# Attention and gated convolution on one core: the order of ReLU and PSUM copies in a step, and the step in which v is loaded

## The chip, the core and the metric

The kernel runs on one core of a Trainium2 chip. The metric is the device time of one execution in microseconds, as the median of several executions. The engines are TensorE (PE; its weight loads are shown as PEld), VectorE (DVE), ScalarE (ACT), GpSimd (POOL) and SyncE (SP), which issues nearly all DMAs. Each engine works through its own queue in order, and a DMA that waits in SP's queue holds up those behind it.

## What is computed

The inputs are q, k and v of shape (4, 8, 576, 64), that is 4 batches of 8 heads, and the weights of a two-layer block. In float32:

```python
q_rot, k_rot = (rotate(q), rotate(k))
scores = scale * np.matmul(q_rot, k_rot.transpose(0, 1, 3, 2))
attn = softmax(scores)                     # over the 576 keys
x = np.matmul(attn, v)                     # heads side by side: (4, 576, 512)
h = np.maximum(x @ w_in, 0.0)              # (4, 576, 1024)
conv_out = sum(conv_w[k] * hp[:, k:k + 576, :] for k in range(3))
out = (h * (1 / (1 + np.exp(-conv_out)))) @ w_out
```

`rotate` is the rotary position turn of the two halves of a head, and `hp` is `h` with a row of zeros on either side.

## The kernel before

The work goes by pairs of heads. There are 16 pairs, and a pair p has five steps, n = 5p to 5p + 4, one for each block of 128 queries (the fifth has 64 queries of both heads). A step multiplies q and k of its block (`emit_S`, L260), reduces the negated maximum on DVE (L268), takes the exponential on ACT (L272), and in the following step PE turns the result `st` round (`emit_T`, L320) into the two tiles `tp`, from which ACT makes two big copies into `pt` (L339, recorded at the helper's line L198, 128x512). Of 576 keys 512 are treated so; the remaining 64 of each head are turned by `emit_Trem` (L357), one block in each of the four steps after the first of a pair. It writes columns 320 to 383 of both PSUM tiles `pm` of the step (`m_pair`), and from there two small copies of 128x64 go into row block 8 of `pt`. They are DVE's, recorded at L200. Five steps after its first, a pair is multiplied with v (`emit_E`, L388): two halves, each into columns 0 to 289 of one `pm` tile, evacuated by ACT (L398).

Up to step 25 PE does attention only, and the weights are converted beside it. From step 26 (`WIDE`) on, the two-layer block is mixed in. Two PSUM tiles `pm` belong to a step, and they are taken anew in the next, so whatever writes them first in a step waits for the last reader of the step before. `UNITS` gives steps with units of the first layer (`emit_M1`, L421): one unit in steps 26 to 34, two in 36, 38, 41, 43, 46, 48 and so on. A unit ends with ReLU on ACT (L429), then convolution on DVE (L433, L435), tanh on ACT (L441), the gate on DVE (L444), and a split into two parts on ACT and POOL (L452, L453). `HALVES` gives the 18 steps with half a second matmul (`m2_half`, L523), whose sum is put together from both tiles by ACT (L537) and DVE (L538). After step 80 comes a tail with the rest of the two layers (L421 and L503 on the tiles `mt`).

What sets the order is a table written by hand: `at(n, rank, fn)` puts a function into step n, and within a step the functions run by rank, equal ranks in the order in which they were entered. Each function issues its instructions to the engines' queues as it runs. `onpe` lists the ranks after which deferred work (`defer`, `tick`) gets its turn. The ranks that matter here, from step 26 on:

- 0: `emit_S`; 0.2: the maximum; 0.3: the convolution of the unit entered last in the step before; 0.45: the transposes of q and k on DVE (L233, L236, L242); 1: `emit_T`; 1.1: `emit_Trem`; 1.5: the exponentials
- 1.6: the two big copies of `tp`; 1.7 and 2.7: the normalisation (L402) and, deferred, its split (L406, L407)
- 2: the units of the first layer; 2.5: the convolution of a first unit of two; 2 and 3: the halves of the second matmul
- 5: the small copies of `pm`; 10: `emit_E`; 18: the rotation of q and k on POOL (L189, L192); 19: loads of q, k (L148 to L150) and v (L160, L161)

Loads of q and k for pair p stand in step n - 10 from step 25 on, and each has one buffer, so it waits until DVE has transposed the pair before. The load of v stands in step n + 3, for use in step n + 5.

Of the kernel before, what the change touches and what calls it, by code (L numbers as in the profile page):

```python
# [20 lines left out]
def attention_moe_kernel(ctx, tc, q, k, v, w_in, conv_w, w_out, tab, tabx, out):  # L21
# [52 lines left out]
    late = {"tail": False, "u": 0}  # L74
# [13 lines left out]
    def t_tile():  # L88
        return psum["t"].tile([128, 512], F32, tag="t", name="tp")

    def after(fn):
        if "m" in psum or late["n"] + 1 == WIDE:
            fn()
        else:
            at(late["n"] + 1, 0.35, fn)

    def spare(n):
        a = free["at"]
        if "m" in psum or late["n"] + 1 == WIDE:
            return t_tile()[:, 0:n]  # L100
        assert a + n <= 960
        free["at"] = a + n
        return free["ps"][:, a:a + n]
# [3 lines left out]
    def m_pair():  # L107
        if pair["n"] != late["n"]:
            pair.update(n=late["n"], ps=[psum["m"].tile([128, 512], F32, tag="m", name="pm") for _ in range(2)], k=0)
        return pair["ps"]  # L110
# [30 lines left out]
    def load(p, part):  # L141
        b, hp = divmod(p, NPB)
        x = raw[p, part] = p1.tile([128, S // 32, 2, 32], F32, tag="r" + part, name="r" + part)
        for h in range(2):
            y = (q if part == "q" else k)[b, 2 * hp + h].rearrange("(c i) d -> i c d", i=32)
            r0 = slice(64 * h, 64 * h + 32)
            r1 = slice(64 * h + 32, 64 * h + 64)
            nc.sync.dma_start(out=x[r0].rearrange("i c e d -> i c (e d)"), in_=y)  # L148
            nc.sync.dma_start(out=x[r1, :, 0, :], in_=y[:, :, 32:64])
            nc.sync.dma_start(out=x[r1, :, 1, :], in_=y[:, :, 0:32])  # L150
# [3 lines left out]
    def load_v(p):  # L154
        if p == 0:
            nc.vector.memset(vrem, 0.0)
        b, hp = divmod(p, NPB)
        t = vmain[p] = p1.tile([128, 2, 4, D], F32, tag="vm", name="vm")
        for h in range(2):
            nc.sync.dma_start(out=t[:, h], in_=v[b, 2 * hp + h, 0:512, :].rearrange("(t p) d -> p t d", p=128))  # L160
            nc.sync.dma_start(out=vrem[64 * h:64 * h + 64, h, :], in_=v[b, 2 * hp + h, 512:S, :])  # L161
# [34 lines left out]
    def evac(eng, out, in_, sc=None):  # L196
        if eng == "A" or "m" not in psum:
            nc.scalar.activation(out=out, in_=in_, func=AF.Copy, scale=1.0 if sc is None else sc)  # L198
        elif sc is None:
            nc.vector.tensor_copy(out, in_)  # L200
        else:
            nc.vector.tensor_scalar(out=out, in0=in_, scalar1=sc, scalar2=None, op0=ALU.mult)
# [110 lines left out]
    def emit_T(p, s, h=None):  # L313
        if not h:
            tps[p] = [t_tile() for _ in range(2)]
        ps = tps[p]

        def turn(k, x, r):
            i = slice(64 * r, 64 * r + 64)
            nc.tensor.transpose(ps[r][:, 64 * k:64 * k + 64], x[i], idf[i, i])  # L320

        if s == 4:
            st = strem[p % 2]
            for t in range(4):
                for r in range(2):
                    turn(t, st[:, 128 * t:128 * t + 128], r)
            for r in range(2):
                turn(4, st[:, 512 - 64 * r:640 - 64 * r], r)
            evac("A", pt[:, 0:9:2, 512:S], ps[0][:, 0:320].rearrange("p (k c) -> p k c", k=5))
            evac("A", pt[:, 1:8:2, 512:S], ps[1][:, 0:256].rearrange("p (k c) -> p k c", k=4))  # L330
            evac("A", pt[64:128, 8, 512:S], ps[1][64:128, 256:320])
        else:
            for t in range(4):
                for r in range(2):
                    turn(2 * t + h, ST[p, s][:, h, 64 * h + 128 * t:64 * h + 128 * t + 128], r)
            def out():
                for r in range(2):
                    c = 128 * s + 64 * r
                    evac("A", pt[:, 0:8, c:c + 64], ps[r].rearrange("p (k c) -> p k c", k=8))  # L339

            if h and "m" in psum:
                at(late["n"], 1.6, out)
            elif h:
                out()

    def emit_Trem(p, s):
        x = ST[p, s].rearrange("p h k -> p (h k)")[:, 512:640]
        dst = pt[:, 8, 128 * s:128 * s + 128]
        if "m" not in psum:
            ps = spare(128)  # L350
            nc.tensor.transpose(ps, x, idf)
            after(lambda: evac("V", dst, ps))
            return
        for r in range(2):
            i = slice(64 * r, 64 * r + 64)
            ps = m_pair()[r][:, 320:384]
            nc.tensor.transpose(ps, x[i], idf[i, i])  # L357
            at(late["n"], 5, lambda dst=dst[:, i], ps=ps: evac("V", dst, ps))

    rb = {}  # L360

# [284 lines left out]
    WIDE = 26  # L646
    UNITS = {n: 1 for n in (26, 27, 28, 29, 31, 32, 33, 34)}
    UNITS.update({n: 2 for n in (36, 38, 41, 43, 46, 48, 51, 53, 56, 58, 61, 63, 66, 69, 71, 74, 77, 79)})
    HALVES = [37, 39, 42, 44, 47, 49, 52, 54, 57, 59, 62, 64, 67, 68, 72, 73, 76, 78]
    plan = {}  # L650
    onpe = (0, 0.2, 0.5, 1, 2, 3, 4, 10)
    engines = {nc.tensor.engine, nc.vector.engine, nc.scalar.engine, nc.gpsimd.engine, nc.sync.engine}

    def at(n, rank, fn):
        plan.setdefault(n, []).append((rank, len(plan.get(n, [])), fn))

    def emit():
        with tc.manual_schedule(engines=engines):
# [17 lines left out]
            for p in range(1, NP):  # L676
                n = STEPS * p
                for i, part in enumerate("qk"):
                    if p > 1:
                        at(n - 10 if n - 10 >= WIDE - 1 else n - 9 + 2 * i, 19, lambda p=p, part=part: load(p, part))  # L680
                    early = n - 10 >= WIDE - 1
                    at(n - 8 + i if early else max(n - 6 + i, 0) if p > 1 else 0, 18, lambda p=p, part=part: rope(p, part))
                    at(n - 5 if early else max(n - 4 + 2 * i, 2), 0.45, lambda p=p, part=part: emit_TQ(p, part))
                at(n + 3, 19, lambda p=p: load_v(p))
            for p in range(NP):
                n = STEPS * p
                for s in range(STEPS):
# [30 lines left out]
            for n, k in UNITS.items():  # L718
                for i in range(k):
                    blk, f = divmod(late["u"], NF)  # L720
                    late["u"] += 1
                    at(n, 2, lambda blk=blk, f=f, last=i == k - 1: emit_M1(blk, f, last))
            for i, n in enumerate(HALVES):
                for k, u in enumerate(m2_half(i // 2, i % 2)):
                    at(n, 2 + k, u)
            n = -1
# [30 lines left out]
            last = LASTB - 1  # L757
# [7 lines left out]
            for u in seq + second + m2_units(t, B * S // 128):  # L765
                u()
                tick()

    emit()


# [48 lines left out]
```

## Time and profile before

| what | us |
|---|---|
| median of 3 runs | 515.12 |
| the three runs | 515.41, 511.5, 515.12 |
| the profiled execution | 510.98 |
| its span, first to last instruction | 509.1 |
| PE busy in the span | 463.4 (91%) |
| DVE busy | 368.3 (72%) |
| ACT busy | 316.4 (62%) |
| POOL busy | 301.6 (59%) |

Times in the profile count from the start of the span. A row of the timeline reads: start, duration, engine, line and operation, output<-inputs by the program's names, shapes, how many instructions are merged, and in brackets the idle time of that engine before it and what ended it. A matmul on PE overlaps its neighbours, so PE can be busy all the time. Steps can be found by their score matmuls: step 26 begins near 127.8 us, step 36 near 179.9, step 47 near 242.3, step 48 near 246.8 and step 49 near 252.0; from 212.6 us on the steps of one pair of heads take 26.65 us.

### The profile page before, as it was taken

To read this page: it belongs to the slowest core of one execution; us is meant where nothing else is said; L and a number is where in the kernel's file an instruction comes from. 1 tells how busy PE (TensorE), PEld (TensorE's weight loads), DVE (VectorE), ACT (ScalarE), POOL (GpSimd) and SP (SyncE) were. 2 spreads that over 40 slices of the span, in tenths; PEclk is the share of its full clock that TensorE was granted. 3 is DMA by queue.
4 is the path that set the end of the run, shared out by engine and by line. 5 is a ranking of instruction groups with operands and counts; after the bars stand their busy time and mean duration, and the time that the engine had idled before them with its cause. 6 is when DMAs were issued, how large, how long until landed. Compare 5 with 4: busy or idle time off the path is not lost.

```text
span 509.1 us, 12329 instructions
## 1 busy us (share of the span) xinstructions
PE 463.4 (91%) x4572; PEld 365.8 (72%) x4572; DVE 368.3 (72%) x731; ACT 316.4 (62%) x839; POOL 301.6 (59%) x479
## 2 busy tenths in 40 slices
PE   1879779796879979999999999999999999999997
PEld 1346446454657758787878796979787878899986
DVE  5699888997496958686877777786776475567931
ACT  2588768786485837676768586767677664234510
POOL 3699978999936667566584838392922122223520
PEclk9979897998999999999999999999999999999999
DMA  8976955843331517160807080716101110100011
GB/s 219 184 142 144 203 135 146 205 114 72 72 71 42 100 32 121 48 116 13 152 14 149 13 147 18 137 26 121 42 25 46 35 36 25 41 23 22 0 48 56
DMA packets 140559, 42.71 MB, mean 84 GB/s; under 512 B 132156, under 2 KB 135252, under 8 KB 140500
## 3 DMA queue, kind: packets, MB, share of 16 engines
q1 hardware_dynamic: 139156, 41.54, 38.8%
q8 instruction: 36, 0.59, 0.5%
q10 hardware_dynamic: 1344, 0.39, 0.3%
q14 instruction: 23, 0.19, 0.1%
HBM read 37.12 MB, written 4.79 MB: 82 GB/s over the span
## 4 chain that ended last, share of the span: by engine, by line
PE 46%; DVE 21%; ACT 16%; POOL 8%; DMA 5%; issue 3%; SPq 2%; DVEq 0%; ACTq 0%; POOLq 0%
PE mt L503 10%; PE pm L388 9%; ACT st L272 8%; PE pm L523 7%; PE sp L260 6%; PE mt L421 6%; DVE negm L268 6%; ACT pt L198 5%; DVE c L435 4%; PE pm L421 3%; POOL rk L189 2%; DMA rq<-q 2%; PE tp L320 2%; POOL rq L189 2%; DVE c L433 2%
## 5 line engine op out<-in xcount | busy, mean ns | idle before, releaser
L268 DVE TENSOR_REDUCE negm<-sp 128x1 f32<-128x576 f32 x144 | 102.1, 745 | 29.3 <-PE sp L260 22.0
L272 ACT ACTIVATE st<-sp,negm 128x576 f32<-128x576 f32 x128 | 93.8, 739 | 38.5 <-DVE negm L268 38.0
L453 POOL TENSOR_TENSOR g<-c,g 128x288 fp32r<-128x288 f32 (+4 forms) x88 | 54.3, 639 | 90.7 <-ACT g L452 90.4
L260 PE MATMUL sp<-kT,qT 64*128 64x288 f32 (+4 forms) x556 | 103.1, 472 | 4.8 <-DVE kT L236 2.8
L198 ACT ACTIVATE pt<-tp 128x512 f32<-128x512 f32 (+3 forms) x176 | 84.1, 530 | 7.4 <-PE tp L320 6.9
L435 DVE SCALAR_TENSOR_TENSOR c<-rr,cw,c 128x288 f32<-128x288 f32 x128 | 78.6, 614 | 4.5
L421 PE MATMUL pm<-xT,winh 128*128 128x290 f32 x352 | 74.5, 305 | 0.0
L260 PEld LDWEIGHTS sp<-kT,qT 64*128 64x128 f32 (+1 forms) x556 | 49.2, 179 | 24.4 <-issue 13.2
L407 POOL TENSOR_TENSOR xT<-xn,xT 128x290 fp32r<-128x290 f32 x32 | 27.9, 879 | 65.5 <-ACT xT L406 65.5
L189 POOL TENSOR_TENSOR rq<-rq,tabt 128x192 f32<-128x192 f32 x90 | 57.6, 675 | 13.7 <-DMA rq<-q 13.7
L189 POOL TENSOR_TENSOR rk<-rk,tabt 128x192 f32<-128x192 f32 x90 | 58.7, 685 | 7.8 <-DMA rk<-k 7.8
L320 PEld LDWEIGHTS tp<-idf,st 64*128 64x128 f32 x1024 | 43.3, 140 | 24.8 <-ACT st L272 13.9
L320 PE MATMUL tp<-idf,st 64*128 64x64 f32 x1024 | 49.1, 228 | 9.9 <-ACT st L272 9.6
L421 PEld LDWEIGHTS pm<-xT,winh 128*128 128x128 f32 x352 | 56.2, 189 | 1.8
L523 PE MATMUL pm<-wouth,g 64*128 64x256 f32 x576 | 56.5, 281 | 0.0
L388 PE MATMUL pm<-pt,vm 128*64 128x290 f32 x368 | 51.3, 411 | 3.5 <-DVE pt L200 1.7
L433 DVE TENSOR_SCALAR c<-rr,cw 128x288 f32<-128x288 f32 x64 | 29.4, 460 | 34.1 <-ACT rr L429 34.1
L523 PEld LDWEIGHTS pm<-wouth,g 64*128 64x128 f32 x576 | 52.6, 186 | 0.0
L421 PE MATMUL pm<-xT,winl 128*128 128x290 f32 x176 | 52.0, 296 | 0.0
L523 PE MATMUL pm<-woutl,g 64*128 64x256 f32 x288 | 49.5, 276 | 0.0
L444 DVE SCALAR_TENSOR_TENSOR c<-c,rr 128x288 f32<-128x288 f32 x64 | 38.0, 615 | 9.4 <-ACT c L441 9.4
L441 ACT ACTIVATE c<-c 128x288 f32<-128x288 f32 x64 | 28.3, 442 | 24.7 <-DVE c L435 24.5
(108 smaller groups left out, 888.5 us busy)
## 6 DMA issues: line engine op xcount, KB each, us to landing
rq<-q SPq DMA_DIRECT2D x30, 144.0 KB
rq<-q SPq DMA_DIRECT2D x60, 72.0 KB
rk<-k SPq DMA_DIRECT2D x30, 144.0 KB
rk<-k SPq DMA_DIRECT2D x60, 72.0 KB
w<-moe_w_in SPq DMA_DIRECT2D x8, 512.0 KB
vm<-v SPq DMA_DIRECT2D x32, 128.0 KB
w<-moe_w_out SPq DMA_DIRECT2D x8, 512.0 KB
rb<-rd SPq DMA_DIRECT2D x16, 144.0 KB
```

The costliest lines, as they stand in the source:

```text
L189: nc.gpsimd.tensor_tensor(out=y, in0=y, in1=tabt[:, a:a + 3], op=ALU.mult)
L198: nc.scalar.activation(out=out, in_=in_, func=AF.Copy, scale=1.0 if sc is None else sc)
L260: nc.tensor.matmul(out=out, lhsT=qt[64 * h:64 * h + 64, c], rhs=kt[64 * h:64 * h + 64, a:a + n], start=True, stop=True)
L268: reds.setdefault((p, s), []).append(lambda: nc.vector.tensor_reduce(out=nm, in_=sc, axis=AX.XY if len(sc.shape) == 3 else AX.X, op=ALU.ma ...
L272: lambda: nc.scalar.activation(out=dst, in_=sc, func=AF.Exp, bias=nm, scale=1.0, accum_out=sm)
L320: nc.tensor.transpose(ps[r][:, 64 * k:64 * k + 64], x[i], idf[i, i])
L388: nc.tensor.matmul(out=xp[64 * h:64 * h + 64, :], lhsT=vmain[p][:, h, i, :] if i < 4 else vrem[:, h, :], rhs=pt[:, 2 * i + h if i < 4 else ...
L421: nc.tensor.matmul(out=ps[:, 0:XW], lhsT=w[:, kk, fs], rhs=xT[:, xs, e, :], start=(i == 0), stop=(i == n - 1))
L435: nc.vector.scalar_tensor_tensor(out=c, in0=r[:, j + e:j + e + HS], scalar=cw[:, 8 * e + f:8 * e + f + 1], in1=c, op0=ALU.mult, op1=ALU.add,)
L453: nc.gpsimd.tensor_tensor(out=lo, in0=c[:, o:o + n], in1=hi.bitcast(F32), op=ALU.subtract)
L503: nc.tensor.matmul(out=ops[tt][:, 0:width], lhsT=g_tile(tt, f, e), rhs=w[:, f, cols], start=(f == 0 and i == 0), stop=(f == NF - 1 and i = ...
L523: nc.tensor.matmul(out=ps[r][:, 0:256], lhsT=g_tile(tt, f, e)[rows], rhs=w[rows, f, cols], start=(f == 0 and i == 0), stop=(f == NF - 1 an ...
```

## The change

The first-layer units of a step with two get ranks 2 and 2.4 in place of 2 and 2, and the big copies of such a step move from 1.6 to 2.2, between the two units. The small copies go from DVE to ACT, at the same rank 5, except in step 26, where they get rank 11, behind `emit_E`. The load of v moves from step n + 3 to n + 2 for the pairs from the sixth on. `onpe` gets the new rank 2.4. In `evac`, "A" is ACT and "V" is DVE.

```diff
@@ -339,7 +339,7 @@
                     evac("A", pt[:, 0:8, c:c + 64], ps[r].rearrange("p (k c) -> p k c", k=8))
 
             if h and "m" in psum:
-                at(late["n"], 1.6, out)
+                at(late["n"], 2.2 if UNITS.get(late["n"]) == 2 else 1.6, out)
             elif h:
                 out()
 
@@ -355,7 +355,7 @@
             i = slice(64 * r, 64 * r + 64)
             ps = m_pair()[r][:, 320:384]
             nc.tensor.transpose(ps, x[i], idf[i, i])
-            at(late["n"], 5, lambda dst=dst[:, i], ps=ps: evac("V", dst, ps))
+            at(late["n"], 5 if late["n"] > WIDE else 11, lambda dst=dst[:, i], ps=ps: evac("A", dst, ps))
 
     rb = {}
 
@@ -648,7 +648,7 @@
     UNITS.update({n: 2 for n in (36, 38, 41, 43, 46, 48, 51, 53, 56, 58, 61, 63, 66, 69, 71, 74, 77, 79)})
     HALVES = [37, 39, 42, 44, 47, 49, 52, 54, 57, 59, 62, 64, 67, 68, 72, 73, 76, 78]
     plan = {}
-    onpe = (0, 0.2, 0.5, 1, 2, 3, 4, 10)
+    onpe = (0, 0.2, 0.5, 1, 2, 2.4, 3, 4, 10)
     engines = {nc.tensor.engine, nc.vector.engine, nc.scalar.engine, nc.gpsimd.engine, nc.sync.engine}
 
     def at(n, rank, fn):
@@ -681,7 +681,7 @@
                     early = n - 10 >= WIDE - 1
                     at(n - 8 + i if early else max(n - 6 + i, 0) if p > 1 else 0, 18, lambda p=p, part=part: rope(p, part))
                     at(n - 5 if early else max(n - 4 + 2 * i, 2), 0.45, lambda p=p, part=part: emit_TQ(p, part))
-                at(n + 3, 19, lambda p=p: load_v(p))
+                at(n + (2 if n >= WIDE - 1 else 3), 19, lambda p=p: load_v(p))
             for p in range(NP):
                 n = STEPS * p
                 for s in range(STEPS):
@@ -719,7 +719,7 @@
                 for i in range(k):
                     blk, f = divmod(late["u"], NF)
                     late["u"] += 1
-                    at(n, 2, lambda blk=blk, f=f, last=i == k - 1: emit_M1(blk, f, last))
+                    at(n, 2 + 0.4 * i, lambda blk=blk, f=f, last=i == k - 1: emit_M1(blk, f, last))
             for i, n in enumerate(HALVES):
                 for k, u in enumerate(m2_half(i // 2, i % 2)):
                     at(n, 2 + k, u)
```

What this does to the queues is shown at three places. A name like `rr_1718` is the result of one ReLU, `tp` the tile of the big copies, `pm` that of units, halves and small copies.

The first is ACT in the steps with half a second matmul and two units that follow each other (47 and 48), before:

```order
L272 ACTIVATE st,sums<-sp,negm 128x576 x2
L198 ACTIVATE pt<-tp 128x8x64 x2
L537 ACTIVATE oh<-pm 128x256
L406 ACTIVATE xT<-xn 128x290
L441 ACTIVATE c<-c 128x288
L406 ACTIVATE xT<-xn 128x290
L272 ACTIVATE st,sums<-sp,negm 128x576 x2
L198 ACTIVATE pt<-tp 128x8x64 x2
L429 ACTIVATE rr_1718<-pm 128x289
L429 ACTIVATE rr_1719<-pm 128x289
L452 ACTIVATE g<-c 128x288 x2
```

and with the change:

```order
L198 ACTIVATE pt<-tp 128x8x64 x2
L537 ACTIVATE oh<-pm 128x256
L406 ACTIVATE xT<-xn 128x290
L198 ACTIVATE pt<-pm 128x64 x2
L441 ACTIVATE c<-c 128x288
L406 ACTIVATE xT<-xn 128x290
L272 ACTIVATE st,sums<-sp,negm 128x576 x2
L429 ACTIVATE rr_1718<-pm 128x289
L198 ACTIVATE pt<-tp 128x8x64 x2
L429 ACTIVATE rr_1719<-pm 128x289
L198 ACTIVATE pt<-pm 128x64 x2
L452 ACTIVATE g<-c 128x288 x2
```

The first ReLU went ahead of the big copies, and two small copies from `pm` came in behind the second ReLU, and in the step before behind the first split L406. On DVE the small copies stood between the convolution and the maximum of the same two-unit step:

```order
L433 TENSOR_SCALAR c<-rr_1718,cw 128x288
L435 SCALAR_TENSOR_TENSOR c<-rr_1718,cw,c 128x288 x2
L200 COPY pt<-pm 128x64 x2
L268 TENSOR_REDUCE negm<-sp 128x1
L433 TENSOR_SCALAR c<-rr_1719,cw 128x288
```

With the change the row of L200 is gone there and everywhere, and the others keep their order.

The second place is ACT in step 26 and the beginning of step 27, before:

```order
L429 ACTIVATE rr_1716<-pm 128x289
L398 ACTIVATE xn<-pm 128x290
L272 ACTIVATE st,sums<-sp,negm 128x576 x2
L198 ACTIVATE pt<-tp 128x8x64 x2
L429 ACTIVATE rr_1717<-pm 128x289
L441 ACTIVATE c<-c 128x288
```

and with the change:

```order
L429 ACTIVATE rr_1716<-pm 128x289
L398 ACTIVATE xn<-pm 128x290
L198 ACTIVATE pt<-pm 128x64 x2
L272 ACTIVATE st,sums<-sp,negm 128x576 x2
L198 ACTIVATE pt<-tp 128x8x64 x2
L429 ACTIVATE rr_1717<-pm 128x289
```

The small copies of step 26 stand behind the evacuation of the product with v (L398).

The third place is SP's queue from the loads of step 25 to the loads of v for step 30. These rows are the same before and with the change:

```order
L148 DMA rk<-k 32x18x64
L149 DMA rk<-k 32x18x32
L150 DMA rk<-k 32x18x32
L148 DMA rk<-k 32x18x64
L149 DMA rk<-k 32x18x32
L150 DMA rk<-k 32x18x32
L160 DMA vm<-v 128x4x64
L161 DMA vr<-v 64x64
L160 DMA vm<-v 128x4x64
L161 DMA vr<-v 64x64
L370 DMA rd<-rt 9x32 x4
```

No other DMA stands between steps 27 and 28, so the load of v keeps its place in the queue, and so it does for the pairs after it; only for the last three pairs does a load of v now stand ahead of one output DMA (L539) that it followed before, since there a step with an output lies between.

## Rows read from the trace of the kernel before

**Rows 1.** The head of the page.

```profile
span 509.1 us, 12329 instructions
```

**Rows 2.** Windows: stretch, length, busy PE, PEld, DVE, ACT, POOL; clock, DMA share, GB/s.

```profile
212.60:345.80 133.20, 130.24 (x1531) 109.81 (x1530) 101.72 (x215) 92.64 (x243) 83.49 (x129) 1.00 0.42 78
```

**Rows 3.** Waits, whole span: engine, line waited for: us in total, times, longest.

```profile
PE pm L357 <- DVE pt L200: 7.6, 10, 1.8
...
PE pm L388 <- DVE pt L200: 1.7, 1, 1.7
...
PE pm L388 <- DMA vm<-v: 1.4, 1, 1.4
```

**Rows 4.** Timeline of PE, rows with idle time before them.

```profile
133.12 2.17 PE L388 MATMUL pm<-pt,vm 128*64 128x290 f32 x16 [1.74 <-DVE pt L200]
...
146.14 0.40 PE L357 MATMUL pm<-idf,st 64*128 64x64 f32 x2 [1.09 <-DVE pt L200]
...
151.24 2.73 PE L388 MATMUL pm<-pt,vm 128*64 128x290 f32 x15 [1.42 <-DMA vm<-v]
...
186.40 1.71 PE L260 MATMUL sp<-kT,qT 64*128 64x288 f32 x7 [1.28 <-ACT st L272]
...
190.62 0.31 PE L357 MATMUL pm<-idf,st 64*128 64x64 f32 x2 [1.77 <-DVE pt L200]
...
254.41 0.31 PE L357 MATMUL pm<-idf,st 64*128 64x64 f32 x2 [0.59 <-DVE pt L200]
```

**Rows 5.** Timeline of steps 48 and 49, ACT, DVE and PE.

```profile
250.38 1.08 ACT L198 ACTIVATE pt<-tp 128x512 f32<-128x512 f32 x2
...
251.33 0.43 ACT L429 ACTIVATE rr<-pm 128x289 f32<-128x289 f32 x1
...
251.87 0.73 DVE L433 TENSOR_SCALAR c<-rr,cw 128x288 f32<-128x288 f32 x1 [1.00 <-ACT rr L429]
...
252.10 0.41 ACT L429 ACTIVATE rr<-pm 128x289 f32<-128x289 f32 x1 [0.34 <-PE pm L421]
...
253.11 0.71 PE L320 MATMUL tp<-idf,st 64*128 64x64 f32 x16
...
254.06 0.34 DVE L200 COPY pt<-pm 128x64 f32<-128x64 f32 x2
```

**Rows 6.** The chain that ended last, 126 to 192 us: start, us, what.

```profile
140.65 0.35 DVE pt L200 x2
...
144.34 0.77 DVE kT L236
...
182.83 0.78 DVE kT L236
```

**Rows 7.** Waits of SP's queue, 126 to 190 us.

```profile
SPq L148 <- DVE kT L242: 10.8, 1, 10.8
```

**Rows 8.** Groups by line and shape, 130 to 420 us: busy us, mean ns.

```profile
L200 DVE COPY pt<-pm 128x64 f32<-128x64 f32 x88 | 15.3, 215 | 4.8 <-ACT rr L429 4.7
...
L198 ACT ACTIVATE pt<-tp 64x64 f32<-64x64 f32 x11 | 2.4, 219 | 0.3
...
L452 ACT ACTIVATE g<-c 128x64 fp32r<-128x64 f32 x8 | 2.0, 246 | 0.0
```

**Rows 9.** Timeline of the end of step 47, DVE, PE and ACT.

```profile
246.53 0.82 DVE L402 TENSOR_TENSOR xn<-xn,rb 128x290 f32<-128x290 f32 x2
...
246.84 0.28 PE L523 MATMUL pm<-wouth,g 64*128 64x256 f32 x1
...
247.06 0.39 ACT L537 ACTIVATE oh<-pm 128x256 f32<-128x256 f32 x1
247.34 0.44 ACT L406 ACTIVATE xT<-xn 128x290 fp32r<-128x290 f32 x1
247.48 0.42 DVE L538 TENSOR_TENSOR oh<-oh,pm 128x256 f32<-128x256 f32 x1
...
248.26 0.22 PE L357 MATMUL pm<-idf,st 64*128 64x64 f32 x1
```

## The prediction

> **What bounds the kernel now.** I read the page's head first: the span is 509.1 us [rows 1], and the profiled execution took 510.98 us, 1.9 us more around the span. Then the windows, to see what the stage with the edited lines has to give. Nothing changes before step 26 (about 127 us), and the tail after 422 us holds none of the edited operations. In the five pairs from 212.6 to 345.8 us TensorE (PE) is busy 130.2 of 133.2 us at a granted clock of 1.00 [rows 2]. There PE is the bound, and all that an edit on ScalarE (ACT) or VectorE (DVE) can return is its idle time.
>
> So the third view is who PE waits for [rows 3]. Ten waits, 7.6 us in all, stand at L357, the transposes of the remaining keys. They wait for L200, DVE's copy out of the tile pair of the step before. One more of 1.7 us is L388 (attention times v) behind the same copy, and one of 1.4 us is L388 behind the load of v. That is 10.7 us together, an upper end for this change. The fourth view, PE's timeline, says where they are [rows 4]: 1.74 in step 26, 1.09 in step 29, 1.42 for v in step 30, 1.77 between steps 36 and 37. The eight others share 7.6 - 1.1 - 1.8 = 4.7 us; one of them (0.59) is in the rows.
>
> **The copy leaves DVE, and ReLU goes ahead.** Step 48 shows the mechanism [rows 5]. ACT makes the two big copies (1.08 us from 250.38), then the first unit's ReLU (251.33). DVE idles 1.00 us for this ReLU and starts the convolution at 251.87; the small copies stand behind it, at 254.06. PE's transposes L320 (0.71 from 253.11) end at 253.82, and L357 then waits 0.59 us, to 254.41 [rows 4]. With the change ACT does the ReLU at 250.4, the big copies until about 251.9, the second ReLU at 252.10, no later than now, since it waits for PE, and then the small copies, done near 253.0. That is 0.8 us before PE asks. The big copies end 0.5 us later than now, but the L320 that needs their tiles starts 1.2 us after that. So the whole wait goes, here and in the seven like it: -4.7 us. Nothing else stands ready to stop PE there: the exponentials end at 250.4 and are used at 253.1.
>
> Between steps 36 and 37 the wait is 1.77 [rows 4]. ACT runs late there, so the later big copies hold L320 itself by some 0.4 us, and I count -1.4.
>
> **The price on ACT.** There are 88 small copies, eight to a pair of heads. DVE takes 215 ns for one. No ACT copy of this shape is in the trace; the nearest are 64x64 from a PSUM tile at 219 ns and 128x64 between SBUF tiles at 246 ns [rows 8]. I take 0.23, near the first: 20.2 us more on ACT in all, 1.8 us in a period of 26.6. ACT is busy 92.6 of 133.2 us now [rows 2], 70%, and goes to 77%; its own idle time hides the copies. The bounds of what reaches PE are 0 and 0.45 us (two copies back to back) in each step that also has half a second matmul, which is rival A. I take 0, and 0.2 us once, in step 80, where no score matmuls stand between the last ReLU and L388.
>
> **Step 26.** Here L388 writes columns 0 to 289 of a tile whose columns 320 to 383 the copy reads, and it waited 1.74 us for the copy [rows 4]. Rank 11 puts the copies behind the evacuation of L388's result, so L388 starts at once. In step 27 the copies stood 0.35 us in front of DVE's reduction [rows 6]; that goes too, and DVE comes to the transpose of k, at 144.34 now, about 1.74 + 0.35 = 2.1 us sooner.
>
> The Trainium skill, PSUM — Partial Sum Buffer, section "PSUM bank collisions raise a hardware error", says that two engines must be kept apart by bank and quadrant, not by address. The 1.74 us on disjoint columns agrees; by address alone this term would be 0. The rule also speaks against the change: in a step with half a second matmul the copy from the second tile must wait for DVE's addition out of that tile.
>
> **What is late next in front.** The waits up to 186 us do not add up, because a chain that is not PE's takes over. SyncE's (SP's) queue stands 10.8 us for that transpose of k [rows 7], then issues six loads of the next k, and only behind them v. In SP's order v stands behind these loads before and after, since they were issued two steps earlier and block the queue: "v a step sooner" moves nothing here. The transpose ends at 145.11 [rows 6] and L388 of step 30 starts at 151.24 [rows 4], 6.1 us later; it will again. So of 1.74, 1.09 and 1.42 only 2.1 us come back, and PE still waits for v, about 2.2 us. From there on loads, rotation on GpSimd, transpose and the next pair's loads follow each other to the transpose at 182.83 [rows 6], and PE's 1.28 us at 186.40 [rows 4] is that chain arriving. None of its pieces changes, so all of it keeps the 2.1. For no other load of v is a wait in the rows; moving those is worth 0.
>
> **Sum.** 2.1 + 1.4 + 4.7 - 0.2 = 8.0 us. Against the profiled execution: 510.98 - 8.0 = 503.0. That execution is like the lowest of the three runs (511.5); the median, 515.12, is 4.1 us above it, and from there the sum gives 507.1. No row says what makes these 4 us. I take the middle, 505.0.
>
> **Rivals.**
> A, given back in the 18 steps with half a second matmul. After PE's last such matmul of step 47 (it starts at 246.84), ACT has the copy L537 (247.06), a split (247.34), then, new, the small copies, the second behind DVE's addition, which ends at 247.90 [rows 9]. By these rows they end near 248.25, and L357 ran at 248.26: no slack. If ACT is late by both, PE loses 0.45 x 18 = 8.1 us, the whole gain: 511 to 515. Half of it leaves 507 to 511. For it: the thin margin. Against it: the first tile is free sooner than the second, and DVE comes sooner to its addition.
> B, slower. The same place, one link more: the split at 247.34 waits for DVE's normalisation, which is queued behind a convolution. If DVE is late, ACT stands at the split, the copies behind it, and PE behind these. It decides once the normalisation ends over 0.7 us after PE's last matmul of the step; now it ends at 247.35 [rows 9], about 0.2 after. With 0.9 us of such delay in the eight steps with a split, 8 x 1.35 + 10 x 0.45 = 15.3 us: 510.98 - 8.0 + 15.3 = 518, from the median 522. Against it: DVE loses the small copies and gets the ReLU 0.9 us sooner.
> C, more: v does come early, the front chain does not bind, and all 10.7 us return: 500 to 504. For it: PE's rows. Against it: SP's wait of 10.8 us and its order.
>
> **How the numbers follow.** The forecast has 0.60, A 0.23, B 0.08, C 0.09. A measurement of this kernel can tell about 1% (5 us) from no change. Of the forecast 0.55 lies over that; with C and 0.04 of A, 0.68 is faster; 0.24 lies within; B is the 0.08 slower. The range runs from C's lower end, 500, to the upper part of A, 512.
>
> **What would show it.** Right: no L357 wait over 0.2 us from 192 us on; the period, 26.65 us now, near 26.05; the convolution of a first unit some 0.9 us sooner; L388 of step 26 without a wait, L388 of step 30 still waiting for v, about 2 us. Wrong: PE waiting for ACT's small copies after half a second matmul (A), ACT idle at the split for DVE (B), v there before step 30 asks for it (C).

## The result, and the profile after

The changed kernel takes 500.32 us (median of four runs, 499.73 to 500.88) against 514.8 us of the kernel before on the same chip (511.5 to 515.41): the ratio is 0.973, with an interval of 0.969 to 0.978. The profiled execution took 499.73 us, 11.25 us less than that of before (510.98). The forecast was 505.0, in a range of 500 to 512, worked out as 8.0 us off the profiled execution.

The head of the page after the change, and the windows of the five pairs that rows 2 showed, cut at the same places of the program (columns as in rows 2; 128.70 us in place of 133.20):

```profile
span 497.9 us, 12391 instructions
...
PE 459.4 (92%) x4572; PEld 361.2 (73%) x4572; DVE 357.4 (72%) x643; ACT 327.0 (66%) x927; POOL 300.2 (60%) x479
```

```profile
207.70:336.40 128.70, 128.70 (x1532) 107.58 (x1532) 98.17 (x177) 97.84 (x283) 83.65 (x130) 1.00 0.43 81
```

PE is busy all the time there, and a pair takes 25.74 us (before 26.65, forecast 26.05). The five pairs are 4.50 us shorter, although PE had only 2.96 us of idle time in them before [rows 2]. ACT carries 97.84 of 128.70 us, 76% (forecast 77%). The small copies appear as a group of ACT's (line, operation, tiles, count | busy us, mean ns):

```profile
L198 ACT ACTIVATE pt<-pm 128x64 f32<-128x64 f32 x88 | 16.9, 230 | 4.1 <-DVE oh L538 3.7
```

A copy takes 230 ns, the value that was taken between 219 and 246 [rows 8]. Next, all rows of PE's timeline from 126 to 420 us with idle time before them. Rows 4 showed six of before's, and there were seven more L357 waits like the last of them; now four places are left in all:

```profile
145.80 0.99 PE L260 MATMUL sp<-kT,qT 64*128 64x288 f32 x5 [0.48 <-ACT str L272]
...
149.37 4.16 PE L388 MATMUL pm<-pt,vm 128*64 128x290 f32 x15 [2.04 <-DMA vm<-v]
...
184.13 1.71 PE L260 MATMUL sp<-kT,qT 64*128 64x288 f32 x7 [0.31 <-ACT st L272]
...
406.20 2.18 PE L388 MATMUL pm<-pt,vm 128*64 128x290 f32 x16 [0.16 <-ACT pt L198]
```

No L357 stands among them. Step 48 of after, to be read against rows 5 (ACT, DVE, then PE at the next step's L357):

```profile
244.63 0.41 ACT L429 ACTIVATE rr<-pm 128x289 f32<-128x289 f32 x1
244.93 1.08 ACT L198 ACTIVATE pt<-tp 128x512 f32<-128x512 f32 x2
...
246.55 0.34 ACT L198 ACTIVATE pt<-pm 128x64 f32<-128x64 f32 x2
```

```profile
245.15 0.49 DVE L433 TENSOR_SCALAR c<-rr,cw 128x288 f32<-128x288 f32 x1
```

```profile
247.25 0.71 PE L320 MATMUL tp<-idf,st 64*128 64x64 f32 x16
247.80 0.23 PE L357 MATMUL pm<-idf,st 64*128 64x64 f32 x2
```

The step began at 241.01. ReLU goes first, the convolution follows 4.14 us after the step's start (before: 251.87 - 246.80 = 5.07), and the small copies end at 246.89, 0.9 us before L357 starts.

To see where the gain lies I read the start of a step's first score matmul (L260) from PE's timeline and cut the span by it. For before and after:

| stretch | before | after | gain | forecast |
|---|---|---|---|---|
| up to step 26 | 127.78 | 127.56 | 0.22 | 0 |
| step 26 to step 37 | 58.62 | 56.57 | 2.05 | 2.1 |
| steps 37 and 38 | 12.29 | 10.56 | 1.73 | 1.4 |
| step 39 to step 79 | 213.01 | 205.58 | 7.43 | 4.7 |
| step 79 to the end | 97.4 | 97.6 | -0.2 | -0.2 |

### The profile page after: what moved, and what is told of

The parts are those of the page before. It is cut to its first block, busy times and chain, and to the rows that moved or that the text cites. A ratio compares the mean times of both kernels' runs of the same rounds, so it can differ in the third digit from the quotient of the medians.

```text
span 497.9 us, 12391 instructions
## 1 busy us (share of the span) xinstructions
PE 459.4 (92%) x4572; PEld 361.2 (73%) x4572; DVE 357.4 (72%) x643; ACT 327.0 (66%) x927; POOL 300.2 (60%) x479
## 4 chain that ended last, share of the span: by engine, by line
PE 65%; DVE 13%; POOL 7%; DMA 4%; SPq 4%; ACT 3%; issue 2%; DVEq 0%; POOLq 0%; ACTq 0%
PE pm L421 12%; PE sp L260 11%; PE pm L523 10%; PE mt L503 10%; PE pm L388 9%; PE mt L421 7%; PE tp L320 5%; DVE negm L268 4%; POOL rq L189 2%; DMA rq<-q 2%; POOL rk L189 2%; POOL rq L192 2%; DVE wt L558 1%; SPq L149 1%; DVE wt L552 1%
## 5 line engine op out<-in xcount | busy, mean ns | idle before, releaser
L260 PE MATMUL sp<-kT,qT 64*128 64x288 f32 (+4 forms) x556 | 101.0, 468 | 3.6 <-DVE kT L236 1.6
L453 POOL TENSOR_TENSOR g<-c,g 128x288 fp32r<-128x288 f32 (+4 forms) x88 | 52.5, 618 | 84.6 <-ACT g L452 84.3
L260 PEld LDWEIGHTS sp<-kT,qT 64*128 64x128 f32 (+1 forms) x556 | 47.5, 178 | 24.8 <-issue 11.1
L320 PEld LDWEIGHTS tp<-idf,st 64*128 64x128 f32 x1024 | 43.1, 140 | 28.6 <-ACT st L272 18.6
L320 PE MATMUL tp<-idf,st 64*128 64x64 f32 x1024 | 49.4, 229 | 12.7 <-ACT st L272 12.7
L189 POOL TENSOR_TENSOR rk<-rk,tabt 128x192 f32<-128x192 f32 x90 | 57.1, 667 | 5.6 <-DMA rk<-k 5.6
L388 PE MATMUL pm<-pt,vm 128*64 128x290 f32 x368 | 52.6, 424 | 2.2 <-DMA vm<-v 2.0
L523 PEld LDWEIGHTS pm<-wouth,g 64*128 64x128 f32 x576 | 48.5, 185 | 0.0
L523 PE MATMUL pm<-woutl,g 64*128 64x256 f32 x288 | 44.0, 277 | 0.0
L433 DVE TENSOR_SCALAR c<-rr,cw 128x288 f32<-128x288 f32 x64 | 28.0, 437 | 21.7 <-ACT rr L429 20.5
L444 DVE SCALAR_TENSOR_TENSOR c<-c,rr 128x288 f32<-128x288 f32 x64 | 35.2, 572 | 9.4 <-ACT c L441 9.4
L388 PEld LDWEIGHTS pm<-pt,vm 128*64 128x64 f32 x368 | 27.2, 142 | 20.1 <-ACT pt L198 2.4
```

The lines of the kernel that those rows point to most:

```text
L189: nc.gpsimd.tensor_tensor(out=y, in0=y, in1=tabt[:, a:a + 3], op=ALU.mult)
L260: nc.tensor.matmul(out=out, lhsT=qt[64 * h:64 * h + 64, c], rhs=kt[64 * h:64 * h + 64, a:a + n], start=True, stop=True)
L388: nc.tensor.matmul(out=xp[64 * h:64 * h + 64, :], lhsT=vmain[p][:, h, i, :] if i < 4 else vrem[:, h, :], rhs=pt[:, 2 * i + h if i < 4 else ...
L453: nc.gpsimd.tensor_tensor(out=lo, in0=c[:, o:o + n], in1=hi.bitcast(F32), op=ALU.subtract)
L523: nc.tensor.matmul(out=ps[r][:, 0:256], lhsT=g_tile(tt, f, e)[rows], rhs=w[rows, f, cols], start=(f == 0 and i == 0), stop=(f == NF - 1 an ...
```

## Experiments

Each kernel was timed in five rounds beside the kernel before on the same chip. The chips differ: the kernel before has a median of 514.8 us beside after, and of 512.5 to 513.1 beside the others, so kernels are compared by their ratios and by the stretches of their profiles. In the table, "26-37", "37-39" and "39-79" are the three middle stretches of the table above, in us, from the profiled execution of each; the starts are read in the same way.

| kernel | median | ratio to before, 95% | 26-37 | 37-39 | 39-79 |
|---|---|---|---|---|---|
| before | 514.8 | | 58.62 | 12.29 | 213.01 |
| after | 500.32 | 0.9731 [0.9688, 0.9775] | 56.57 | 10.56 | 205.58 |
| a_copies | 502.95 | 0.9805 [0.9781, 0.9830] | 57.48 | 11.89 | 205.50 |
| b_relu | 503.30 | 0.9817 [0.9793, 0.9842] | 58.81 | 11.75 | 205.52 |
| c_v | 513.12 | 1.0004 [0.9986, 1.0022] | 58.97 | 12.22 | 212.94 |
| d_before | 512.84 | 0.9997 [0.9978, 1.0017] | 59.09 | 14.00 | 212.75 |
| e_rank5 | 504.34 | 0.9838 [0.9808, 0.9869] | 58.94 | 10.56 | 205.50 |
| f_dve | 511.60 | 0.9971 [0.9953, 0.9989] | 59.03 | 12.22 | 211.34 |
| g_twice | 505.08 | 0.9849 [0.9822, 0.9875] | 56.86 | 12.07 | 207.53 |
| h_tk | 498.15 | 0.9703 [0.9681, 0.9725] | 54.48 | 11.63 | 205.58 |
| j_vfirst | 500.69 | 0.9763 [0.9736, 0.9790] | 56.50 | 10.57 | 205.58 |
| k_tk8 | 498.35 | 0.9715 [0.9689, 0.9741] | 55.52 | 9.55 | 205.59 |
| l_both | 494.80 | 0.9632 [0.9604, 0.9660] | 51.41 | 9.55 | 205.59 |

**The parts alone.** Four kernels ran together: the small copies on ACT alone, the order of ReLU alone, the load of v alone, and the kernel before unchanged.

a_copies, the kernel before with

```diff
-            at(late["n"], 5, lambda dst=dst[:, i], ps=ps: evac("V", dst, ps))
+            at(late["n"], 5 if late["n"] > WIDE else 11, lambda dst=dst[:, i], ps=ps: evac("A", dst, ps))
```

> Only the small copies go to ScalarE (rank 5, and 11 in step 26); ReLU order and load of v as before. Theory (the wait was the copies' place behind the convolution in VectorE's queue): this part alone frees them, since on ScalarE they stand behind the second ReLU, which ends at 252.5 in step 48, so they end near 252.9 and PE asks at 253.65. It also holds the step 26 term of about 2. Expected nearly the whole effect: no L357 wait on VectorE, span 11 us shorter, 500 to 504 us. Rival (the parts add up, and the earlier ReLU is what shortens the path): about half, 507 to 509 us, with waits left at L357 in the two-unit steps.

b_relu, the kernel before with

```diff
-                at(late["n"], 1.6, out)
+                at(late["n"], 2.2 if UNITS.get(late["n"]) == 2 else 1.6, out)
...
-    onpe = (0, 0.2, 0.5, 1, 2, 3, 4, 10)
+    onpe = (0, 0.2, 0.5, 1, 2, 2.4, 3, 4, 10)
...
-                    at(n, 2, lambda blk=blk, f=f, last=i == k - 1: emit_M1(blk, f, last))
+                    at(n, 2 + 0.4 * i, lambda blk=blk, f=f, last=i == k - 1: emit_M1(blk, f, last))
```

> Only the order in the two-unit steps: first ReLU ahead of the big copies, small copies still on VectorE. Theory: the convolution starts 0.9 us sooner, the small copies behind it end near 252.8 in place of 254.4, and PE asks at 253.65, so the waits of the two-unit steps go here too (about 6 us by the differences between the starts of steps, and most of the 1.8 us after step 36), but the front part of 2 us stays: 507 to 509 us, span 501 to 503. Rival (only moving the copies off VectorE counts): no change, 511 to 515 us.

c_v, the kernel before with

```diff
-                at(n + 3, 19, lambda p=p: load_v(p))
+                at(n + (2 if n >= WIDE - 1 else 3), 19, lambda p=p: load_v(p))
```

> Only the load of v a step sooner. Theory: SyncE's queue is blocked by the loads of k, v keeps its place, nothing changes: ratio to before 1.00 within 0.4%, and L388 of step 30 still waits 1.4 us for v. Rival (v does arrive sooner): that wait gone, 1 to 2 us less.

d_before has no edit.

> The kernel before, unchanged, against itself: ratio 1.00. The question is its spread of 4 us (511.5 to 515.4), of which the changed kernel shows 1 us. Theory: the spread is in the front part, where the granted clock falls, and the spans and clocks of the single executions go together. Rival: the long executions have the same clock and lose time elsewhere.

The stretch from 39 to 79, eight pairs of heads in their steady order, is clear: 205.50 with the copies alone, 205.52 with the ReLU alone, 205.58 with both. Each part alone takes all of it, so the two don't add up: alone they take 1.95% and 1.83% off the time, which would be 3.8% together, where both took 2.7%. In steps 37 and 38 neither alone (11.89, 11.75) gives what both give (10.56). For the ReLU it goes with the clock (last section). With the copies alone step 38 takes 6.30 us against 5.20 with both. There the first ReLU of step 36 still stands behind the big copies, DVE waits 1.94 us for it, and ACT comes late to all that follows, into step 38. First ACT in a_copies, then PE:

```profile
192.14 1.08 ACT L198 ACTIVATE pt<-tp 128x512 f32<-128x512 f32 x2
...
193.70 0.51 ACT L198 ACTIVATE pt<-pm 128x64 f32<-128x64 f32 x2
```

```profile
193.28 0.75 PE L320 MATMUL tp<-idf,st 64*128 64x64 f32 x15
194.00 0.54 PE L357 MATMUL pm<-idf,st 64*128 64x64 f32 x2
```

The step began at 191.58. L320 goes on as the big copies end (193.22), and the two L357 start just behind the ends of the two small copies, the later of which ends at 194.21. L357 starts 2.42 us after the step's start, against 1.47 in after. No idle time of PE is recorded for it, and yet the step is 1.1 us longer. In this one step PE is held by the late big copies and, behind half a second matmul, by the small ones, as rival A had it; with the earlier ReLU, in after, it is not.

The load of v alone is nothing, and its wait stands as before, in c_v:

```profile
151.99 2.71 PE L388 MATMUL pm<-pt,vm 128*64 128x290 f32 x15 [1.40 <-DMA vm<-v]
```

The front is the copies' part: with the ReLU alone step 26 keeps its wait, and 26-37 stays at 58.81. With the copies alone the wait is gone, but 26-37 falls only to 57.48, by 1.14 of the 2.05: the first transpose of k comes as in after (14.81 and 14.87 us after the start of step 26), the last one 0.9 us later (53.90 and 52.99). Why was not followed up. First PE in b_relu, then in a_copies:

```profile
133.12 2.17 PE L388 MATMUL pm<-pt,vm 128*64 128x290 f32 x16 [1.73 <-DVE pt L200]
...
186.59 1.85 PE L260 MATMUL sp<-kT,qT 64*128 64x288 f32 x7 [1.68 <-ACT st L272]
```

```profile
150.29 4.01 PE L388 MATMUL pm<-pt,vm 128*64 128x290 f32 x15 [2.07 <-DMA vm<-v]
...
185.99 1.72 PE L260 MATMUL sp<-kT,qT 64*128 64x288 f32 x7 [2.01 <-ACT st L272]
```

The repeat of before says something on the spread of its times (511.5 to 515.41). Its profile differs from the first one mostly in steps 37 and 38, 14.00 against 12.29 us. PE waited 1.93 us at the start of step 37 and 0.89 at its L357 (first profile: 1.28 and 1.77 [rows 4]), and here the granted clock fell behind it. Over the twelve executions of d_before the mean clock does not go with the time, though: the longest (514.84 us) has 0.979, the shortest (510.96) 0.980. What makes the spread stays open. The windows (stretch, length, busy PE, clock, DMA share, GB/s):

```profile
180.00:190.00 10.00, 8.07 (x74) 0.91 0.07 21
190.00:200.00 10.00, 9.11 (x97) 0.75 1.04 157
```

**The bank, and the place in the queue.** e_rank5 is the changed kernel with

```diff
-            at(late["n"], 5 if late["n"] > WIDE else 11, lambda dst=dst[:, i], ps=ps: evac("A", dst, ps))
+            at(late["n"], 5, lambda dst=dst[:, i], ps=ps: evac("A", dst, ps))
```

> The changed kernel, but the small copies of step 26 at rank 5 (ahead of the evacuation of the attention product) in place of 11; still on ScalarE. Theory (a tile's bank is held as a whole, so L388 waits for a copy of other columns; and the chain from step 26 through the loads passes the delay on): L388 of step 26 waits 1.5 to 1.8 us for the small copy, and the total is 1.0 to 2.0 us above the changed kernel's 500.3, near 502. Rival (the columns are disjoint, or ScalarE comes early enough): no wait, same time within 0.4 us.

```profile
134.26 2.17 PE L388 MATMUL pm<-pt,vm 128*64 128x290 f32 x16 [1.57 <-ACT pt L198]
```

The wait is back, now for ACT's copy, and 26-37 is 2.4 us longer than in after (58.94 against 56.57): 1.6 us more in step 26 and 1.7 more in step 36, whose end waits for the chain (2.04 against 0.31 us at step 37), less 1.0 in step 30. The whole is 4.0 us by the medians, twice the expected 1.0 to 2.0; of the difference of the profiled executions, 3.8 us, 1.5 us already lay ahead of step 26, where nothing was edited. The direction is shown, the total is not.

f_dve is the kernel before with the small copies still on DVE, but ahead of the convolution in steps with two units:

```diff
-            at(late["n"], 5, lambda dst=dst[:, i], ps=ps: evac("V", dst, ps))
+            at(late["n"], 2.45 if UNITS.get(late["n"]) == 2 else 5, lambda dst=dst[:, i], ps=ps: evac("V", dst, ps))
```

> The kernel before with one edit: in steps with two units the small copies, still on VectorE, get rank 2.45, ahead of the first unit's convolution, in place of 5; the ReLU stays behind the big copies. Theory (the copies' place in VectorE's queue behind the convolution made the L357 waits, not the engine): no L357 wait from 192 us on above 0.2 us, front as before, about 503.5 to 505. Rival (a convolution that starts later pushes the units and gives the gain back, or the engine matters): 508 or above.

Here my theory fell and the rival held: 511.6 us, 1.3 below before. The L357 waits of 0.3 to 0.9 us in the steps after those with two units are gone, and yet 39-79 is 211.34. DVE in step 48, which begins at 246.94 here:

```profile
252.51 0.23 DVE L200 COPY pt<-pm 128x64 f32<-128x64 f32 x1 [0.93 <-ACT rr L429]
253.14 0.23 DVE L200 COPY pt<-pm 128x64 f32<-128x64 f32 x1 [0.40 <-ACT rr L429]
253.28 0.58 DVE L433 TENSOR_SCALAR c<-rr,cw 128x288 f32<-128x288 f32 x1
```

Each copy waits for the ReLU that reads other columns of its tile, and the convolution stands behind both: it starts 6.34 us after the step's start, 1.27 later than before. What DVE does in the next step comes later by it, the addition L538 and the copies behind it too, and PE loses 0.2 us at the L357 of the two-unit step itself, which had no wait before, and 0.23 to 0.28 at L388 in each of steps 45, 50, 55, 60 and 65. By the starts of steps, step 48 is 0.45 and step 50 0.27 us longer than before, and step 49 0.78 shorter. The waits at L357 (columns of the waits, 212 to 400 us):

```profile
PE pm L357 <- DVE pt L200: 1.4, 7, 0.2
```

So a copy ahead of the convolution on DVE only trades one wait for another. What helps is that the copies leave DVE, or that the ReLU comes early enough for all that stands behind it.

**The copies' price on ACT.** g_twice is the changed kernel with every small copy issued twice.

```diff
             at(late["n"], 5 if late["n"] > WIDE else 11, lambda dst=dst[:, i], ps=ps: evac("A", dst, ps))
+            at(late["n"], 5 if late["n"] > WIDE else 11, lambda dst=dst[:, i], ps=ps: evac("A", dst, ps))
```

> The changed kernel with every small copy made twice on ScalarE, 88 copies more, at some 0.12 to 0.23 us each 10 to 20 us more of ScalarE's time. Theory (ScalarE's own idle time hides them, also in the 18 steps with half a second matmul): no wait of TensorE for a small copy over 0.2 us from 192 us on, total 0 to 1.5 us above the changed kernel's 500.3. Rival (no slack there: the small copies end just as TensorE asks, so a second pair of 0.35 us reaches the end in each of the 18 steps): 4 to 7 us more, 504.5 to 507.

The total, 505.08, lies in the rival's 504.5 to 507, but only part of it stands where the rival puts it. From step 39 to 79 the second pair of copies costs 207.53 - 205.58 = 1.95 us. It stands in eight steps, 43, 48, 53, 58, 63, 68, 73 and 77, each right behind a step with half a second matmul, with 0.19 to 0.36 us in each; behind the other nine such steps it is 0.13 us at most. No wait is recorded for it. Step 48, ACT and then PE:

```profile
244.46 0.84 ACT L198 ACTIVATE pt<-pm 128x64 f32<-128x64 f32 x4
```

```profile
245.35 0.27 PE L357 MATMUL pm<-idf,st 64*128 64x64 f32 x1
```

The fourth copy ends at 245.30, and the second L357 starts 0.05 us later, 1.71 us after the step's start. In after the copies of this step end at 242.30 and the second L357 starts at 242.56, 1.55 after the step's start. So the small copies have 0.26 us to spare there, and a second pair takes more than that. The next largest piece is in steps 37 and 38 (12.07 against 10.56), where PE had waited 1.40 at the start of step 37 and the clock was 0.66 from 185 to 190 us; the remaining 1.0 us lies ahead of step 37, 0.7 of it before step 26. Neither expectation was right: one pair of copies is hidden from step 39 to 79, a second pair is not in eight of these 40 steps.

**The wait for v.** i_v put the load of v between the loads of q and k of step 25:

```diff
-                        at(n - 10 if n - 10 >= WIDE - 1 else n - 9 + 2 * i, 19, lambda p=p, part=part: load(p, part))
+                        at(n - 10 if n - 10 >= WIDE - 1 else n - 9 + 2 * i, 19 + 0.4 * i * (p == 7), lambda p=p, part=part: load(p, part))
...
-                at(n + (2 if n >= WIDE - 1 else 3), 19, lambda p=p: load_v(p))
+                at(25 if p == 5 else n + (2 if n >= WIDE - 1 else 3), 19.2 if p == 5 else 19, lambda p=p: load_v(p))
```

> The changed kernel with the load of v of one pair (the sixth) put into SP's order between the loads of q and of k of step 25, so that it does not stand behind the k loads that wait for VectorE's transpose; nothing else moves. Theory (the chain of loads, rotation and transposes holds step 37): L388 of step 30 waits less than 0.3 us, no clock below 1.00 at 148 to 156 us, steps 31 to 35 some 3 to 4 us sooner, but S of step 37 within 0.5 us of before, total 499.8 to 500.5. Rival (the wait for v and the low clock after it reach the end): 496 to 498.5.

It told nothing on the question. The last 64 rows of v have one buffer, so in this kernel the product of step 26 takes the rows of the next pair, and PE waits for them:

```profile
137.23 1.92 PE L388 MATMUL pm<-pt,vr 128*64 128x290 f32 x4 [4.41 <-DMA vr<-v]
```

It took 507.53 us (0.9886 of before, 0.9867 to 0.9904). j_vfirst asks the same without this: the changed kernel with the eighth pair's loads of k behind the load of v in step 27.

```diff
-                        at(n - 10 if n - 10 >= WIDE - 1 else n - 9 + 2 * i, 19, lambda p=p, part=part: load(p, part))
+                        at(n - 10 + 2 * i * (p == 7) if n - 10 >= WIDE - 1 else n - 9 + 2 * i, 19 + 0.4 * i * (p == 7), lambda p=p, part=part: load(p, part))
```

> The changed kernel with the six loads of one pair's k (the eighth) put behind the load of v in SP's order in step 27, so that v doesn't stand behind loads that wait for VectorE's transpose; nothing else moves. Theory (TensorE's wait for v and the low clock after it are hidden by the chain of loads, rotation and transposes that sets S of step 37): no wait for v at L388 of step 30, clock near 1.00 at 148 to 156 us, S of step 31 two to four us sooner, but S of step 37 within 0.5 us and the total 499.5 to 500.8. Rival (the wait and the clock after it reach the end): 496 to 498.5.

The wait for v is gone and the clock stays up; then PE loses the time at the next places, and 26-37 is 56.50 against 56.57. The windows of after and of j_vfirst, then PE in j_vfirst:

```profile
148.00:156.00 8.00, 6.63 (x31) 0.57 0.16 33
```

```profile
148.00:156.00 8.00, 8.00 (x76) 1.00 0.08 12
```

```profile
158.87 1.71 PE L260 MATMUL sp<-kT,qT 64*128 64x288 f32 x7 [2.35 <-ACT st L272]
...
184.62 1.72 PE L260 MATMUL sp<-kT,qT 64*128 64x288 f32 x7 [1.47 <-ACT st L272]
```

Step 31 starts 4.5 us sooner than in after, step 37 0.5 us later, which is the 0.5 it was behind from the start. That is the chain that the prediction spoke of: an earlier PE only waits longer for it.

**The chain itself.** Its pieces in after, from the chain that ended last, 126 to 192 us:

```profile
149.11 3.56 POOL rk L189 x6
152.67 1.65 POOL rk L192 x3
154.34 0.78 DVE kT L236
...
160.62 0.53 SPq L148
...
163.36 3.31 DMA rq<-q
166.82 4.08 POOL rq L189 x6
...
178.87 1.66 POOL rk L192 x3
180.55 0.78 DVE kT L236
...
182.57 0.65 DVE negm L268
183.25 0.84 ACT st L272 x2
184.13 1.71 PE sp L260 x7
```

The transpose at 180.55 is for step 40; it has no business ahead of step 36's maximum, but stands there in DVE's queue. So there are two handles: start the chain sooner (h_tk), or take its end out of PE's way (k_tk8).

```diff
-                    at(n - 5 if early else max(n - 4 + 2 * i, 2), 0.45, lambda p=p, part=part: emit_TQ(p, part))
+                    at(n - 5 if early else max(n - 4 + (1 if p == 6 else 2) * i, 2), 0.45, lambda p=p, part=part: emit_TQ(p, part))
```

> The changed kernel with the transpose of the second k of one pair (the seventh) put one step sooner, into step 27 in place of 28; nothing else moves. Theory (the chain from VectorE's transpose through SP's loads, the rotation and the next transposes holds the front, TensorE only follows): transposes after it come 3.5 to 4 us sooner, v is there before step 30 asks, no clock below 1.00 at 148 to 156 us, S of step 37 3 to 4 us sooner, total about 496.5. Rival (another link, TensorE or POOL, takes over at once): less than 1 us gained, 499.5 to 500.3.

```diff
-                    at(n - 5 if early else max(n - 4 + 2 * i, 2), 0.45, lambda p=p, part=part: emit_TQ(p, part))
+                    at(n - 5 + (i if p == 8 else 0) if early else max(n - 4 + 2 * i, 2), 0.45, lambda p=p, part=part: emit_TQ(p, part))
```

> The changed kernel with VectorE's transpose of k of one pair (the ninth) one step later, in step 36 in place of 35, behind the maximum of step 36; nothing else moves. Theory (what holds step 37 is that the maximum of step 36 stands on VectorE behind this transpose, which waits for the rotation on GpSimd): no idle time of VectorE before that transpose, the 0.3 us wait at S of step 37 goes and the steps 36 and 37 take 0.4 and 0.8 us less, total 498.8 to 499.8. Rival (another link, the exponentials or the loads, holds the step): 500.0 to 500.8.

l_both has both edits.

> Both moves of VectorE's transposes together: k of the seventh pair one step sooner (27), k of the ninth one step later (36). Theory (each alone leaves the other link; with both, TensorE runs through from step 31, which the first move alone already brought 5.7 us sooner): S of step 37 four to five us sooner than in the changed kernel, no clock below 0.9 from 148 us on, total 494 to 496. Rival (a third link, the loads behind the normalisation's sums, takes the gain): 497 to 498.5, as with the first move alone.

h_tk gained less than forecast, 498.15. PE was 5.7 us ahead at step 31, but at step 37 only 2.5, held by the same link, and behind that wait the granted clock fell (0.68 from 180 to 185 us):

```profile
181.59 2.53 PE L260 MATMUL sp<-kT,qT 64*128 64x288 f32 x7 [2.17 <-ACT st L272]
```

k_tk8 went below its range, 498.35: 1.05 us off 26-37 and 1.0 off steps 37 and 38, which now take 9.55. Of the 1.05, 0.64 is step 30, where the clock was 0.79 from 148 to 156 us against 0.57 in after. By their intervals neither of the two kernels is clear of the changed one; it is the stretches that show the gain, with 39-79 the same in all. With both, l_both takes 494.8 us (492.73 to 494.86): 51.41 and 9.55. DVE's idle time ahead of the two transposes is gone, and PE runs through; the only wait that the view of PE's waits shows from 126 to 420 us is this, in step 80:

```profile
PE pm L388 <- ACT pt L198: 0.2, 1, 0.2
```

Its interval, 0.960 to 0.966 of before, lies below that of the changed kernel, 0.969 to 0.978, so it is faster than that too. From step 26 to 39 the first move alone gains 1.0 us on after, the second 2.1, both together 6.2 (67.13 against 60.96): two links of one chain.

## Why the prediction was right, and where not

- **Faster, and by the mechanism named: right.** The L357 waits are gone, the first unit's convolution comes 0.93 us sooner (forecast: some 0.9), and L388 of step 26 starts at once. But two edits serve one wait: a_copies and b_relu show that either would have done from step 39 to 79. The prediction worked them as one and could not tell.
- **The front, 2.1 us: right, 2.05.** That it came within 0.05 is luck: the same stretch takes 58.97 in c_v and 59.09 in the repeat of before, against 58.62, and the copies alone gave 1.14. The chain came as forecast: the transpose of k at 142.43 for 144.34, 1.9 us sooner, and L388 of step 30 6.2 us after its end (forecast 6.1). Right too was that v would still be waited for (forecast: about 2.2 us at 149.2; found: 2.04 at 149.37), that moving its load is worth nothing (c_v), and that this chain is not PE's (j_vfirst).
- **Steps 37 and 38, 1.4: too low by 0.3**, found 1.73. The 0.4 us subtracted for big copies that come late on ACT did show, as 0.3, though no idle time over 0.1 us is recorded there. L320 goes on when these copies end, 186.13 - 184.13 = 2.00 us after the start of step 37, and before 188.10 - 186.40 = 1.70. What was missing is the overlap of the next point: in this step L357 starts 0.22 us before L320 ends, and 1.77 + 0.22 - 0.30 = 1.69 of the 1.75 us by which step 37 is shorter. In k_tk8, where ACT is in time, step 37 takes another 0.93 us less. L320 in before, then in after:

```profile
188.10 0.75 PE L320 MATMUL tp<-idf,st 64*128 64x64 f32 x15
```

```profile
186.13 0.71 PE L320 MATMUL tp<-idf,st 64*128 64x64 f32 x15
186.62 0.22 PE L357 MATMUL pm<-idf,st 64*128 64x64 f32 x1
```

- **The eight waits from step 39 to 79, 4.7: this is the term that failed.** Found: 7.43. The prediction took PE's idle time for all that an edit can return, and 10.7 us, the sum of the waits that it found, for an upper end; the profiled execution fell by 11.25, with 2.35 us of waits for v and for the chain still there. In those eight steps the time from one step's start to the next falls by 6.06 us, against 4.78 us of recorded idle time. The reason lies in the rows: unhindered, L357 starts before the last L320 has ended. In after it starts at 247.80, and L320 ends at 247.25 + 0.71 = 247.96, an overlap of 0.16. In before, as the prediction has it, L320 ended at 253.82, and L357 started 0.59 us later [rows 4]. The wait cost 0.59 + 0.16 = 0.75, and step 49 became 0.78 shorter. In after the overlap is 0.16 or 0.17 in all eight steps, and eight times 0.16 make the missing 1.3. The other 1.4 us are gains of at most 0.15 in steps without any recorded wait; what they are stays open.
- **ACT's price, 0.23 each and hidden: right** (230 ns). The 0.2 us in step 80 is no loss: 0.16 is recorded there, and before had 0.20 at the same place for a ReLU; the 0.2 us lost after step 79 lie elsewhere in the tail and were not followed up. Rival A is out for the changed kernel: no L357 behind half a second matmul waits for the copies. Its thin margin was real, though: 0.26 us in step 48, where a second pair of copies overran it (g_twice), and in step 38 of a_copies the copies came too late. The second copy does wait for DVE's addition, 0.4 us at most. Its waits from 190 to 412 us:

```profile
ACT pt L198 <- DVE oh L538: 3.7, 10, 0.4
```

- **Rival B is out** (there is no wait of PE behind ACT's split), and **C in its mechanism too**: v does not come early. Its band of 500 to 504 holds the time all the same, because the period gave more.
- **The rule of the bank.** Step 26 (e_rank5, 1.57 us) and the copies that wait for ReLU (f_dve) are waits between disjoint columns of one tile. The Trainium skill, PSUM — Partial Sum Buffer, section "PSUM bank collisions raise a hardware error", asks for engines to be kept apart by bank and quadrant, not by address, and these waits agree with it. They are waits that the program makes; what the chip would do without them was not tried.
- **The starting point.** 505.0 was the middle between 503.0, from the profiled execution, and 507.1, from the median. With the right size of the period (7.4 for 4.7, and 0.3 more in steps 37 and 38) the profiled execution gives 500.0, and 499.73 was measured. The median of 500.32 lies 0.3 us above the lower end of the range, and that end came from rival C; that the range holds it is luck. The 4 us above it did not come along: the runs of the changed kernel lie within 1.2 us. One source of longer times is seen, steps 37 and 38 of d_before with their lower clock (1.7 us); whether the highest runs come from it too was not seen, since no profile of one exists.

## What to carry to other kernels

Where PE is the bound, an idle time that the profile records for it is the least that a wait costs: add the overlap that the same pair of instructions has in a step without the wait, and compare the starts of steps, since in these runs PE also lost up to 1.1 us in a step with no idle time recorded. Where another chain is the bound, a wait of PE costs nothing, as the 2.04 us for v did (j_vfirst). When two edits cure one wait, time each alone, since their gains need not add up. And look in the queue of a waiting engine for work that is not due yet: moving two transposes by a step each brought 5.5 us more by the medians, without a single operation fewer.

## What was not expected of the hardware

A short idle time of PE can cost more than itself. Behind the 2.04 us for v in after, the granted clock was 0.57 from 148 to 156 us, and the product of step 30 took 8.05 us (from 149.37 to step 31 at 157.42), against 157.08 - 151.24 = 5.84 in before at 1.00. The same happened at step 37: b_relu waited 1.68 there and had 0.51 from 188 to 191 us, f_dve 1.92 and 0.55, the repeat of before 1.93 and 0.75, g_twice 1.40 and 0.66, h_tk 2.17 and 0.68. But it need not: a_copies waited 2.01 and e_rank5 2.04 there, c_v 1.82 and j_vfirst 1.47, and all four kept 1.00, as the first profile of before did (1.28). At the wait for v its length does not decide either: a_copies (2.07) and e_rank5 (2.21) had 0.72 over the 6 us around it, g_twice (2.22) kept 1.00. What decides was not found. In after (0.31), k_tk8 and l_both (none) no such fall was seen at step 37. For b_relu the rows are these (windows as above):

```profile
185.00:188.00 3.00, 1.41 (x7) 1.00 0.02 2
188.00:191.00 3.00, 3.00 (x35) 0.51 0.46 127
191.00:194.00 3.00, 3.00 (x46) 0.92 1.06 182
```
